# Block 0's score bursts on 32x64 array tiles: 16 full bursts in place of 18, with the output products half way between them

## The chip, the cores and the metric

The kernel runs on one core of a Trainium2 chip. The metric is device time in microseconds (us), taken by the median of several runs. The engines are PE (TensorE, matrix products), PEld (its weight loads, which overlap the products), DVE (VectorE), ACT (ScalarE), POOL (GpSimd) and SP (SyncE, which issues transfers).

## The reference

It is one transformer layer for 2048 tokens of width 1024, in bf16: a sliding-window causal attention with 32 heads of width 32 and window 256, then a feed-forward part.

```python
def _A_ref(x, wqkv, wo):                       # x is layernormed
    H = 32; Dh = D // H; W = 256
    q, k, v = ...                              # from x @ wqkv
    scores = jnp.einsum("bhqd,bhkd->bhqk", q, k) * (Dh ** -0.5)
    mask = (i - j >= 0) & (i - j < W)          # i query, j key
    p = _softmax(jnp.where(mask, scores, -1e9))
    o = jnp.einsum("bhqk,bhkd->bhqd", p, v)
    return o.reshape(B, S, D) @ wo
h  = x + _A_ref(_layernorm(x), wqkv, wo)
h2 = h + silu(_layernorm(h) @ w1) @ w2
```

## The kernel before

The 2048 tokens are four blocks of 512. TensorE works through the dense products of the next block (Q, K, V), 192 products of 512 columns for a block. Between them, in bursts, it computes the attention scores of the block before, and in pieces the attention outputs. A head group is four heads; their contractions are 32 long, so four row tiles of the array hold one head each. A burst fills two tiles in PSUM, the memory that TensorE writes: `sc[0]` and `sc[1]`, each with 512 columns for two heads (the text calls them the score banks). ScalarE takes the exponential into SBUF, GpSimd masks the triangles there, and TensorE later multiplies by V.

Block 0 has no keys before it, and had its own code: chunks of 128 keys by 128 queries, strung together over head groups, four to a burst.

```python
def first_stream(n_groups):
    bursts, where = [], {}
    for g in range(n_groups):
        for kt, q in ((0, 0), (0, 1), (0, 2), (1, 1), (1, 2), (1, 3), (2, 2), (2, 3), (3, 3)):
            if not bursts or len(bursts[-1]) == 4:
                bursts.append([])
            ...
def scores_first(n):
    ...                                       # nq: chunks in a row with the same keys
            for hh in range(4):
                r0 = hh * DH
                nc.tensor.matmul(
                    sc[hh // 2][:, hh % 2, ch * P:(ch + nq) * P],
                    lhsT=kT[0][r0:r0 + DH, g, kt * P:(kt + 1) * P],
                    rhs=qT[0][r0:r0 + DH, g, q0 * P:(q0 + nq) * P],
                    start=True, stop=True, tile_position=(r0, 0))
    for pair in range(2):
        e = ebuf[(2 * n + pair) % 12]          # a ring of six bursts
        nc.scalar.activation(out=e, in_=sc[pair], func=ACT.Exp, scale=scale)
        ...                                    # masks on GpSimd
```

An output piece (18 products of 33 columns: two heads, four query tiles) ran directly behind a burst:

```python
def between(kt):                               # called ahead of every dense product
    k, m = count
    if m * len(first_bursts) >= k * 192:
        run_late()
        scores_first(k)
        if pending:
            pending.pop(0)()
        ...
```

Blocks 1 to 3 already used 64-key halves on 32x64 tiles (`scores_xy`, with a burst of 128-key chunks, `scores_c`, for every second head group), a ring `xy_ring` of four bursts, a ring `c_ring` of three groups, and pieces half way between bursts.

The softmax here doesn't subtract the row's maximum and nothing guards it: scores larger than these inputs give would overflow.

## Time and profile before

| | before |
|---|---|
| time, median | 693.77 us (3 runs, 693.46 to 695.77); 693.63 us with three more |
| TensorE busy | 687.3 us, 99% of the span of 691.9 us |
| ScalarE, GpSimd busy | 240.8 us (35%), 161.8 us (23%) |
| stage of block 0 (first burst to first burst of the next stage) | 55.64 us |
| in it | 192 dense products, 18 bursts, 14 output pieces |

Read it so: with TensorE busy all the time, a stage is as long as the list of TensorE's instructions in it. The timeline gives each term by the difference of two starts. The lines are in the prediction below.

### The profile page before, as it was taken

To read this page: it belongs to the slowest core of one execution; us is meant where nothing else is said; L and a number is where in the kernel's file an instruction comes from. 1 tells how busy PE (TensorE), PEld (TensorE's weight loads), DVE (VectorE), ACT (ScalarE), POOL (GpSimd) and SP (SyncE) were. 2 spreads that over 40 slices of the span, in tenths; PEclk is the share of its full clock that TensorE was granted. 3 is DMA by queue.
4 is the path that set the end of the run, shared out by engine and by line. 5 is a ranking of instruction groups with operands and counts; after the bars stand their busy time and mean duration, and the time that the engine had idled before them with its cause. 6 is when DMAs were issued, how large, how long until landed. Compare 5 with 4: busy or idle time off the path is not lost.

```text
span 691.9 us, 13823 instructions
## 1 busy us (share of the span) xinstructions
PE 687.3 (99%) x5859; PEld 330.1 (48%) x5859; DVE 292.5 (42%) x616; ACT 240.8 (35%) x400; POOL 161.8 (23%) x295
## 2 busy tenths in 40 slices
PE   8999999999999999999999999999999999999998
PEld 3444445555555555544444444444444444444445
DVE  6267646744444449543315133343133251333111
ACT  4326656666766676521310033300133100233000
POOL 1007666656666665500000000000000000000000
PEclk9999999999999999999999999999999999999999
DMA  7732231236462999971023410023200023100110
GB/s 243 259 60 72 33 93 54 26 63 174 81 131 18 228 248 276 228 267 46 16 76 109 98 38 1 1 91 70 84 0 1 17 94 94 39 1 1 30 39 24
DMA packets 76462, 60.93 MB, mean 88 GB/s; under 512 B 50288, under 2 KB 60528, under 8 KB 76400
## 3 DMA queue, kind: packets, MB, share of 16 engines
q1 hardware_dynamic: 76256, 59.78, 33.1%
q8 instruction: 46, 0.75, 0.5%
q10 hardware_dynamic: 144, 0.26, 0.1%
q14 instruction: 16, 0.13, 0.1%
HBM read 39.85 MB, written 8.39 MB: 70 GB/s over the span
## 4 chain that ended last, share of the span: by engine, by line
PE 99%; DMA 0%; DVE 0%; issue 0%
PE hacc L615 19%; PE hacc L652 17%; PE acc L250 16%; PE acc L652 10%; PE acc L615 9%; PE acc L240 8%; PE acc L271 7%; PE o_ps L377 4%; PE sc L302 3%; PE hacc L271 1%; PE o_ps L392 1%; PE sc L348 1%; PE sc L328 1%; DMA r_o<-in_A_x_dram 0%; PE tp L218 0%; DVE ln_st L171 0%
## 5 line engine op out<-in xcount | busy, mean ns | idle before, releaser
L368 POOL TENSOR_SCALAR_AFFINE_SELECT r_e<-r_e 128x512 bf16<-128x512 bf16 (+1 forms) x288 | 158.8, 570 | 125.7 <-ACT r_e L357 64.7
L652 PEld LDWEIGHTS <-r_a 128*128 128x128 bf16 x952 | 90.9, 98 | 103.0
L615 PEld LDWEIGHTS <-r_w 128*128 128x128 bf16 x896 | 87.5, 98 | 105.0
L652 PE MATMUL hacc<-r_a 128*128 128x512 bf16 (+2 forms) x616 | 122.5, 360 | 0.0
L615 PE MATMUL hacc<-r_e,r_w 128*128 128x512 bf16 x456 | 100.9, 379 | 0.0
L314 ACT ACTIVATE r_e<-sc 128x768 bf16<-128x768 f32 x96 | 78.2, 814 | 48.3 <-PE sc L302 48.3
L624 ACT ACTIVATE r_n<-hacc 128x512 f32<-128x512 f32 x30 | 17.9, 597 | 178.9 <-PE hacc L615 178.9
L652 PE MATMUL acc<-r_a 128*128 128x512 bf16 x336 | 74.0, 379 | 0.0
L250 PEld LDWEIGHTS <-r_w 128*128 128x128 bf16 x512 | 45.0, 97 | 47.3 <-issue 0.2
L252 DVE CAST r_a<-acc 128x512 bf16<-128x512 f32 x56 | 38.6, 690 | 57.1 <-PE acc L250 56.9
L250 PE MATMUL acc<-r_t,r_w 128*128 128x512 bf16 x256 | 61.7, 379 | 0.0
L250 PE MATMUL acc<-r_w 128*128 128x512 bf16 x256 | 59.9, 379 | 0.0
L271 PE MATMUL acc<-r_o,r_a 128*128 128x512 bf16 x208 | 51.9, 379 | 0.0
L615 PE MATMUL acc<-r_e,r_w 128*128 128x512 bf16 x216 | 49.1, 379 | 0.0
L377 PEld LDWEIGHTS <-r_e 128*128 128x128 bf16 x1152 | 37.8, 96 | 14.2
L357 ACT ACTIVATE r_e<-sc 128x1024 bf16<-128x1024 f32 x36 | 34.9, 1021 | 21.2 <-PE sc L348 20.1
L377 PE MATMUL o_ps<-r_a,r_e 128*128 128x33 bf16 x1152 | 38.3, 178 | 0.0
L667 DVE SCALAR_TENSOR_TENSOR r_t<-hacc,r_t 128x512 bf16<-128x512 f32 (+2 forms) x22 | 14.0, 635 | 56.4 <-PE hacc L652 56.4
L315 ACT ACTIVATE r_e<-sc 128x256 bf16<-128x256 f32 x96 | 37.4, 390 | 0.0
L667 DVE SCALAR_TENSOR_TENSOR r_t<-acc,r_t 128x512 bf16<-128x512 f32 x12 | 8.3, 691 | 64.2 <-PE acc L652 64.2
L625 DVE SCALAR_TENSOR_TENSOR r_a<-r_n,hacc 128x512 bf16<-128x512 f32 x30 | 20.6, 688 | 33.0 <-ACT r_n L624 33.0
L615 PE MATMUL hacc<-r_a,r_w 128*128 128x512 bf16 x144 | 32.9, 379 | 0.0
(75 smaller groups left out, 529.0 us busy)
## 6 DMA issues: line engine op xcount, KB each, us to landing
r_w<-in_B_w_dram SPq DMA_DIRECT2D x8, 896.0 KB, 5.5
r_a<-in_B_w_dram SPq DMA_DIRECT2D x7, 1024.0 KB, 7.8
r_w<-in_A_wqkv_dram SPq DMA_DIRECT2D x6, 1024.0 KB, 8.6
h_dram<-r_t SPq DMA_DIRECT2D x16, 256.0 KB, 3.3
r_t<-h_dram SPq DMA_DIRECT2D x16, 256.0 KB, 2.9
out_dram<-r_t SPq DMA_DIRECT2D x31, 128.0 KB, 1.7
r_o<-in_A_x_dram SPq DMA_DIRECT2D x15, 256.0 KB, 3.6
r_e<-h_dram SPq DMA_DIRECT2D x3, 1024.0 KB, 5.7
```

Source lines behind the costliest of these rows:

```text
L240: nc.tensor.matmul(acc, lhsT=lnT_b[b % 2][:, kt, j * P:(j + 1) * P], rhs=wv[:, kt, c * 512:(c + 1) * 512], start=(kt == 0), stop=(kt == KT ...
L250: nc.tensor.matmul(acc, lhsT=wqk[:, kt, col0:col0 + P], rhs=lnT_b[b % 2][:, kt, :], start=(kt == 0), stop=(kt == KT - 1))
L252: copy(out=(qT, kT)[which][b][:, g, :], in_=acc)
L271: nc.tensor.matmul(acc, lhsT=qT[b][:, g, j * P:(j + 1) * P], rhs=wo[:, g, c * 512:(c + 1) * 512], start=(g == 0), stop=(g == G - 1))
L314: nc.scalar.activation(out=tri[:, :, :, 64:256], in_=both, func=ACT.Exp, scale=scale)
L315: nc.scalar.activation(out=e[:, 1024:1280].rearrange("p (h q) -> p h q", q=P), in_=bank[:, :, 192:320], func=ACT.Exp, scale=scale)
L357: nc.scalar.activation(out=e, in_=sc[pair], func=ACT.Exp, scale=scale)
L368: nc.gpsimd.affine_select(out=dst, in_=src, pattern=[[0, n] for n in dst.shape[1:-1]] + [[sgn, P]], compare_op=ALU.is_ge if upper else ALU ...
L377: nc.tensor.matmul(o_ps[pair][:, qt * 2 + hh, 0:VW], lhsT=chunk_of(i, bank, piece, pair, hh), rhs=v[:, b * 4 + kt, g * 4 + pair * 2 + hh, ...
L615: nc.tensor.matmul(acc, lhsT=w1[:, kt, ft * P:(ft + 1) * P], rhs=ln2T[b][:, kt, :], start=(kt == 0), stop=(kt == KT - 1))
L652: nc.tensor.matmul(acc[:, 0:c1 - c0], lhsT=gT[:, ft, j * P:(j + 1) * P], rhs=w2[ft // 4][:, ft % 4, c0:c1], start=(ft == 0), stop=(ft == F ...
L667: nc.vector.scalar_tensor_tensor(out=t_out[j % 2][:, c0:c1], in0=acc[:, 0:c1 - c0], scalar=0.5, in1=t_in[j % 2][:, c0:c1], op0=ALU.mult, o ...
```

## The change

Its intent is to give block 0 the scheme of the other blocks. With 64-key halves, columns that the mask removes need not be computed, and a head group fits into exactly two bursts of 512 columns, 16 in all. Pieces go half way between bursts. The deferred output transposes (`run_late`) also move: they are issued ahead of each eight dense products instead of ahead of each burst.

```diff
+CHUNKS_0 = [
+    [(0, "X", 0)],
+    [(0, "X", 1), (1, "Y", 0)],
+    [(0, "X", 2), (1, "Y", 1), (2, "X", 3)],
+    [(1, "Y", 2), (2, "C", 1), (3, "Y", 3)],
+]
-def first_stream(n_groups): ...
-    def scores_first(n): ...
+    def scores_0(g, odd):
+        q0 = odd * P
+        parts = [
+            (odd, 0, q0, q0 + 320, 0), (odd, 1, q0, q0 + 384, 0),
+            (odd + 2, 0, q0 + 256, 448, 320), (odd + 2, 1, q0 + 320, 448, 384),
+        ]
+        if odd:
+            parts = [(a, h, f, min(t, 512), c) for a, h, f, t, c in parts[:2]] + [
+                (3, 0, 384, 512, 320), (3, 1, 448, 512, 384), (2, 0, 448, 512, 448), (2, 1, 448, 512, 448)]
+        for step in range(0, len(parts), 2):
             for hh in range(4):
+                for t, half, qa, qb, col in parts[step:step + 2]:
+                    r0 = hh * DH
+                    k0 = t * P + half * 64
+                    nc.tensor.matmul(
+                        sc[hh // 2][half * 64:half * 64 + 64, hh % 2, col:col + qb - qa],
+                        ..., tile_position=(r0, half * 64),
+                    )
         for pair in range(2):
+            e = xy_ring[(g % 2 * 2 + odd) * 2 + pair][:, 0:1024].rearrange("p (h q) -> p h q", q=512)
+            nc.scalar.activation(out=e[:, :, 0:256], in_=sc[pair][:, :, 0:256], ...)
+            nc.scalar.activation(out=e[:, :, 320:512], in_=sc[pair][:, :, 256:448], ...)
+            nc.scalar.activation(out=c_ring[...], in_=sc[pair][:, :, 448:512], ...)
+            select(...)  # three masks of 256 columns
-    def attn_out_first(g, pair): ...
     class Stream:
         def __init__(self, b):
+            self.behind = 2 if b else 1
+            pending.extend(coming)
+            coming.clear()
         def between(self, kt):
-            if self.seen * 20 >= self.done * 192:
+            if self.seen * self.n >= self.done * 192:
                 self.bursts[self.done]()
                 self.done += 1
-            if self.seen * 40 >= (self.given * 2 + 1) * 192:
+            if self.seen * self.n * 2 >= (self.given * 2 + 1) * 192:
                 if pending:
                     pending.pop(0)()
-                coming.append(...)
-                if len(coming) > 2:
+                coming.append(self.pieces[self.given])
+                if len(coming) > self.behind:
                     pending.append(coming.pop(0))
...
-    def between(kt): ...
+    stream = Stream(0)
```

More of the change, by code (lines that the diff above doesn't have):

```diff
@@ L32 @@
 ]
-SPLIT = [(0, 8), (8, 16), (16, 21), (21, 27), (27, 32)]
-def first_stream(n_groups):
-    bursts, where = [], {}
-    for g in range(n_groups):
-        for kt, q in ((0, 0), (0, 1), (0, 2), (1, 1), (1, 2), (1, 3), (2, 2), (2, 3), (3, 3)):
-            if not bursts or len(bursts[-1]) == 4:
-                bursts.append([])
-            where[g, kt, q] = (len(bursts) - 1, len(bursts[-1]))
-            bursts[-1].append((g, kt, q))
-    return bursts, where
+CHUNKS_0 = [
[4 more added lines that the diff above has]
+]
+SPLIT = [(0, 8), (8, 16), (16, 21), (21, 27), (27, 32)]
 @with_exitstack
@@ L125 @@
     w2 = [view(r_a, w2_off + 4096 * s, 4, D) for s in W2_SLOT]
-    ebuf = [view(r_e, 1024 * i, 2, 512) for i in range(12)]
     c_ring = view(r_e, 0, 3, 4, 256)
@@ L160 @@
     make_identity(nc, ident[:])
-    warm = ebuf[0]
+    warm = view(r_e, 0, 2, 512)
     nc.vector.memset(warm, 0.0)
@@ L281, in chunk_of @@
             return c_ring[:, (i + 1) % 3, pair * 2 + hh, piece * P:(piece + 1) * P]
-        c0 = 1024 + hh * P if piece == 2 else hh * 512 + (piece - piece // 3) * P
+        if i < G:
+            c0 = hh * 512 + piece * P
+        else:
+            c0 = 1024 + hh * P if piece == 2 else hh * 512 + (piece - piece // 3) * P
         return xy_ring[(i % 2 * 2 + "XY".index(bank)) * 2 + pair][:, c0:c0 + P]
-    first_bursts, first_where = first_stream(G)
     def scores_xy(b, g, odd):
@@ L337, in scores_c @@
                                  in_=sc[pair].rearrange("p h (n q) -> p n h q", q=256), func=ACT.Exp, scale=scale)
-    def scores_first(n):
-        ch = 0
-        while ch < 4:
-            g, kt, q0 = first_bursts[n][ch]
-            nq = 1
-            while ch + nq < 4 and first_bursts[n][ch + nq] == (g, kt, q0 + nq):
-                nq += 1
-            for hh in range(4):
-                r0 = hh * DH
-                nc.tensor.matmul(
-                    sc[hh // 2][:, hh % 2, ch * P:(ch + nq) * P],
-                    lhsT=kT[0][r0:r0 + DH, g, kt * P:(kt + 1) * P],
-                    rhs=qT[0][r0:r0 + DH, g, q0 * P:(q0 + nq) * P],
-                    start=True, stop=True, tile_position=(r0, 0),
-                )
-            ch += nq
-        for pair in range(2):
-            e = ebuf[(2 * n + pair) % 12]
-            nc.scalar.activation(out=e, in_=sc[pair], func=ACT.Exp, scale=scale)
-            for ch, (g, kt, q) in enumerate(first_bursts[n]):
-                if kt != q - 1:
-                    mask(e, ch, 1, kt == q)
@@ L362, in mask @@
-    def mask(e, c0, n, upper):
-        for_each = e[:, :, c0 * P:(c0 + n) * P].rearrange("p h (c q) -> p h c q", q=P)
-        select(for_each, for_each, upper)
+    def scores_0(g, odd):
[8 more added lines that the diff above has]
+        for step in range(0, len(parts), 2):
+            for hh in range(4):
+                for t, half, qa, qb, col in parts[step:step + 2]:
[3 more added lines that the diff above has]
+                        sc[hh // 2][half * 64:half * 64 + 64, hh % 2, col:col + qb - qa],
+                        lhsT=kT[0][r0:r0 + DH, g, k0:k0 + 64],
+                        rhs=qT[0][r0:r0 + DH, g, qa:qb],
+                        start=True, stop=True, tile_position=(r0, half * 64),
+                    )
+        for pair in range(2):
+            e = xy_ring[(g % 2 * 2 + odd) * 2 + pair][:, 0:1024].rearrange("p (h q) -> p h q", q=512)
+            nc.scalar.activation(out=e[:, :, 0:256], in_=sc[pair][:, :, 0:256], func=ACT.Exp, scale=scale)
+            nc.scalar.activation(out=e[:, :, 320:512], in_=sc[pair][:, :, 256:448], func=ACT.Exp, scale=scale)
+            nc.scalar.activation(out=c_ring[:, (g + 1) % 3, pair * 2:pair * 2 + 2, 128 + 64 * odd:192 + 64 * odd],
+                                 in_=sc[pair][:, :, 448:512], func=ACT.Exp, scale=scale)
+            select(e[:, :, 0:P], e[:, :, 0:P], True)
+            select(e[:, :, 256:384], e[:, :, 320:448], False)
+            select(e[:, :, 384:512], e[:, :, 384:512], True)
@@ L375, in attn_out @@
             pair, qt, hh = n // 8, n // 2 % 4, n % 2
-            for m, (kt, bank, piece) in enumerate(CHUNKS[qt]):
+            chunks = (CHUNKS if b else CHUNKS_0)[qt]
+            for m, (kt, bank, piece) in enumerate(chunks):
                 nc.tensor.matmul(
@@ L380, in attn_out @@
                     rhs=v[:, b * 4 + kt, g * 4 + pair * 2 + hh, :],
-                    start=(m == 0), stop=(m == 2),
+                    start=(m == 0), stop=(m == len(chunks) - 1),
                 )
@@ L384, in attn_out @@
                 attn_norm(i, pair)
-    def attn_out_first(g, pair):
-        for qt in range(4):
-            for hh in range(2):
-                kts = range(max(0, qt - 2), qt + 1)
-                for kt in kts:
-                    n, ch = first_where[g, kt, qt]
-                    nc.tensor.matmul(
-                        o_ps[pair][:, qt * 2 + hh, 0:VW],
-                        lhsT=ebuf[(2 * n + pair) % 12][:, hh, ch * P:(ch + 1) * P],
-                        rhs=v[:, kt, g * 4 + pair * 2 + hh, :],
-                        start=(kt == kts[0]), stop=(kt == qt),
-                    )
-        attn_norm(g, pair)
-        if pair == 1:
-            late.append(lambda: attn_transpose(0, g))
     def attn_norm(i, pair):
@@ L428, in __init__ @@
         def __init__(self, b):
-            self.b, self.bursts, self.done, self.given, self.seen = b, [], 0, 0, 0
+            self.bursts, self.pieces, self.done, self.given, self.seen = [], [], 0, 0, 0
+            self.behind = 2 if b else 1
+            pending.extend(coming)
+            coming.clear()
             for g in range(0, G, 2):
-                self.bursts += [lambda g=g: scores_c(b, g)]
-                self.bursts += [lambda g=g, k=k, o=o: scores_xy(b, g + k, o) for k in range(2) for o in range(2)]
+                if b:
+                    self.bursts += [lambda g=g: scores_c(b, g)]
+                    self.bursts += [lambda g=g, k=k, o=o: scores_xy(b, g + k, o) for k in range(2) for o in range(2)]
+                    self.pieces += [lambda g=g, s=s: attn_piece(b, g, *s) for s in SPLIT]
+                else:
+                    self.bursts += [lambda g=g, k=k, o=o: scores_0(g + k, o) for k in range(2) for o in range(2)]
+                    self.pieces += [lambda g=g, k=k: attn_piece(b, g, k, k + 8) for k in range(0, 32, 8)]
+            self.n = len(self.bursts)
         def between(self, kt):
-            if self.seen * 20 >= self.done * 192:
+            if self.seen * self.n >= self.done * 192:
                 self.bursts[self.done]()
                 self.done += 1
-            if self.seen * 40 >= (self.given * 2 + 1) * 192:
+            if self.seen * self.n * 2 >= (self.given * 2 + 1) * 192:
                 if pending:
                     pending.pop(0)()
-                coming.append(lambda b=self.b, n=self.given: attn_piece(b, n // 5 * 2, *SPLIT[n % 5]))
-                if len(coming) > 2:
+                coming.append(self.pieces[self.given])
+                if len(coming) > self.behind:
                     pending.append(coming.pop(0))
@@ L523 @@
     pending, coming = [], []
-    count = [0, 0]
-    def between(kt):
-        k, m = count
-        if m * len(first_bursts) >= k * 192:
-            run_late()
-            scores_first(k)
-            if pending:
-                pending.pop(0)()
-            for g in range(G):
-                if first_where[g, 3, 3][0] == k:
-                    pending.extend([lambda g=g: attn_out_first(g, 0), lambda g=g: attn_out_first(g, 1)])
-            count[0] += 1
-        count[1] += 1
-    dense = [lambda j=j, c=c: v_group(1, j, c, dve, between) for j in range(4) for c in range(2)]
-    dense += [lambda w=w, g=g: qk_group(1, w, g, dve, between) for g in range(G) for w in range(2)]
+    stream = Stream(0)
+    dense = [lambda j=j, c=c: v_group(1, j, c, dve, stream.between) for j in range(4) for c in range(2)]
+    dense += [lambda w=w, g=g: qk_group(1, w, g, dve, stream.between) for g in range(G) for w in range(2)]
     for n in range(24):
+        run_late()
         dense[n]()
@@ L546 @@
             turns.pop(0)()
-    assert not steps and not turns and count[0] == len(first_bursts)
+    assert not steps and not turns
     for b in range(2, NB):
```

## The prediction

> **What bounds the kernel now.** I read the head of the page first, then its chain, then the timeline of TensorE in the stage that the change touches, then the same stage's waits, and last the stage of block 1, which already works the way that block 0 is to work.
>
> ```profile
> PE 687.3 (99%) x5859; PEld 330.1 (48%) x5859; DVE 292.5 (42%) x616; ACT 240.8 (35%) x400; POOL 161.8 (23%) x295
> ...
> PE 99%; DMA 0%; DVE 0%; issue 0%
> ```
>
> TensorE is busy 99% of the span, and the chain that ended last is TensorE for 99% too. So time goes down only where TensorE's own instruction stream gets shorter, and goes up where that stream gets longer or has to wait. ScalarE (35%) and GpSimd (23%) matter only if they make TensorE wait.
>
> The stage of block 0 begins with its first burst of scores and ends at the first burst of block 1's stage. The timeline of TensorE (start, length, line, output and inputs, count) shows its rhythm:
>
> ```profile
> 50.58 0.40 PE L348 MATMUL sc<-r_a 32*128 32x384 bf16 x8
> 50.91 2.55 PE L240 MATMUL acc<-r_w,r_t 128*128 128x512 bf16 x11
> 53.39 0.40 PE L348 MATMUL sc<-r_a 32*128 32x256 bf16 x8
> ...
> 58.79 0.40 PE L348 MATMUL sc<-r_a 32*128 32x384 bf16 x8
> 59.12 0.62 PE L392 MATMUL o_ps<-r_a,r_e 128*128 128x33 bf16 x18
> 59.59 2.53 PE L240 MATMUL acc<-r_w,r_t 128*128 128x512 bf16 x11
> 62.06 0.40 PE L348 MATMUL sc<-r_a 32*128 32x128 bf16 x12
> ...
> 106.22 0.40 PE L328 MATMUL sc<-r_a 32*128 32x128 bf16 x16
> ```
>
> L240 and L250 are the dense products of block 1, L348 a burst, L392 an output piece (18 products of 33 columns). Lengths overlap, so I use starts. The stage lasts 106.22 - 50.58 = 55.64 us. In an undisturbed stretch 50 dense products take 10.8 us, 0.216 us each, so the stage's 192 take 41.5 us. A burst takes 0.33 us from its start to the next instruction's (50.58 to 50.91); 11 dense products need 2.38 us, but from 50.91 to 53.39 are 2.48 us, so about 0.10 us goes by in front of each burst. A burst is 0.43 us. A piece takes 59.59 - 59.12 = 0.46 to 0.47 us; fourteen of the sixteen run in this stage, two after it. Sum: 41.5 + 18 x 0.43 + 14 x 0.46 = 41.5 + 7.7 + 6.4 = 55.6 us. That is the whole stage: it has no stall that a better order could win back.
>
> The waits of this stage name no wait of TensorE's products. What is there is the other engines waiting for TensorE, and a small wait of a weight load:
>
> ```profile
> ACT r_e L357 <- PE sc L348: 20.1, 17, 1.5
> ...
> PEld L392 <- POOL r_e L368: 0.4, 2, 0.2
> ```
>
> **What the Trainium skill says.** "TensorEngine Tiling (Array Packing)", section Tiling Modes, Key Properties, says that a change of tiling mode drains TensorE and that tiles work independently. The trace agrees with both: 0.10 us is lost in front of a burst, and a burst that streams four times 512 columns on four row tiles takes 0.33 us where one dense product of 512 takes 0.216. "TensorE: Matmul & The Clock Gate", section Back-to-back issue gap, gives N/2.4 + 2.5 ns, so 216 ns for 512 columns; the trace has 216. The same page, Part 3, section The mechanism, says that products start and end strictly in program order; nothing in the trace before tests this, since its 64-key bursts have halves of equal length in every step, and I use it only as a risk below.
>
> **The change part by part.**
>
> *Fewer bursts.* Before, a head group has 9 chunks of 128 keys by 128 queries, 1152 columns a head; 72 chunks fill 18 bursts of 512 columns. After, 64-key halves skip what the mask removes, and a group needs two bursts of 512 columns: 16 bursts. At 0.43 us this removes 2 x 0.43 = 0.86 us of TensorE. Most of it isn't streaming: 512 columns are 0.213 us, the rest is going into the small tiles and out.
>
> *Dearer bursts.* The 16 bursts run on 32x64 tiles and have 16 products (even) or 24 (odd), 320 in all where 168 were. Block 1's stage prices such a burst:
>
> ```profile
> 123.10 1.24 PE L240 MATMUL acc<-r_w 128*128 128x512 bf16 x5
> 124.27 0.43 PE L302 MATMUL sc<-r_a 32*64 32x320 bf16 x24
> 124.62 1.25 PE L240 MATMUL acc<-r_w 128*128 128x512 bf16 x5
> 125.71 0.61 PE L377 MATMUL o_ps<-r_a,r_e 128*128 128x33 bf16 x18
> 126.17 0.38 PE L240 MATMUL acc<-r_w 128*128 128x512 bf16 x1
> ```
>
> Five dense products end at 123.10 + 1.08 = 124.18, so 0.09 us in front, then 0.35 to 0.36 us: 0.45 us for 24 products and also 512 columns a half. That is 0.02 dearer than 0.43. The even burst has fewer products but unequal halves (320 and 384 columns, then 192 and 128). If products must start in order, a head's 192-column product can't start before its neighbour's second half does at column 384, and it ends at 576 instead of 512: 64 columns or 0.027 us more. So 0.45 to 0.47 us a burst, and 16 x 0.02 to 16 x 0.04 = 0.3 to 0.6 us back.
>
> *Outputs moved.* The pieces keep their size: per pair 2 x (1 + 2 + 3 + 3) = 18 products, 288 in all, and again 14 in the stage and two handed over. In front of them now stand dense products. The same lines show a piece of 18 there: 126.17 - 125.71 = 0.46 us, with the five dense before it at 1.09 instead of 1.08. So moving costs or wins under 0.01 us a piece; the burst's exit is paid towards a dense product instead.
>
> *ScalarE.* A burst had two exponentials of 1024 columns (1.94 us together, 51.01 to 52.95); now it has six, of 512, 384 and 128 columns twice. Block 1's four (768 and 256 twice) run from 118.87 to about 120.93, 2.06 us: 0.06 us for each further instruction. Six would take about 2.17 us (estimate). They start some 0.6 us after the burst's start (118.28 to 118.87), so the score banks are free 2.8 us after it. Bursts will stand 12 x 0.216 + 0.45 = 3.04 us apart without a piece and 3.5 us with one. TensorE doesn't wait.
>
> *GpSimd.* 96 masks of 256 columns before (6 of 9 chunks, 2 pairs, 8 groups), 96 after (3 x 2 x 16), at 0.42 us: 2.5 us a burst, inside 3.04 us. The mask results are wanted 1.5 burst intervals after their burst, over 4.5 us; pair 0's masks should be done after 0.6 + 1.1 + 1.3 = 3.0 us.
>
> *Sum.* 0.86 away, 0.3 to 0.6 back, at most 0.1 for the pieces: 0.2 to 0.5 us less, 0.4 taken. 693.77 - 0.4 = 693.4 us, 0.06% of the time.
>
> **Rivals.**
> 1. ScalarE becomes the stage's bound through its two score banks, which are not doubled. For it: block 1's stage shows such a stall. Where two bursts stood close, the second took 0.65 us instead of 0.36:
>
> ```profile
> 112.35 0.43 PE L302 MATMUL sc<-r_a 32*64 32x320 bf16 x24
> 112.71 2.12 PE L240 MATMUL acc<-r_w 128*128 128x512 bf16 x9
> 114.76 0.72 PE L302 MATMUL sc<-r_a 32*64 32x320 bf16 x24
> 115.41 1.25 PE L240 MATMUL acc<-r_w 128*128 128x512 bf16 x5
> ```
>
> Their starts lie 2.41 us apart, and 0.29 us of stall makes the shortest possible distance 2.70 us. Against it: with two more exponentials that becomes about 2.8 us, and the new bursts are never under 3.0 apart. If I am wrong by 0.3 us a burst, 16 bursts cost 5 us and the time is 698. That stall itself stays, as block 1's stage begins with the same two pieces and the same gap.
> 2. Ring or mask waits: the results now lie in a ring of four bursts, not six. Against it: the last piece that reads a slot runs half an interval (over 1.5 us) before the burst that refills it, and masks have over 1 us to spare. A few waits of 0.2 us make 694 to 695.
> 3. The move wins more, since the piece no longer directly follows a burst: 0.1 us won at each of 14 pieces would be 1.4 us more, so 692. Against it: a piece costs 0.46 us in both places.
>
> **Range and chances.** All terms are a few tenths of a microsecond; the three runs before span 693.46 to 695.77. From the sum, with run-to-run spread and a little for rival 2, I take 692.6 to 694.4. 2% is 13.9 us, a quarter of the whole stage: neither 18 bursts at 0.43 us nor rival 1 reaches it.
>
> **What would show it.** In the profile after: 16 bursts of 16 and 24 products, 3.04 us apart at first and 3.5 later; each 0.35 to 0.38 us from start to next start; pieces of 0.46 us; the stage 55.1 to 55.4 us long, against 55.64; summed busy time of ScalarE up, with waits for TensorE still in front of it; no wait of TensorE for ScalarE or GpSimd. I am wrong if a burst takes over 0.5 us, if a stall like the one at 114.76 shows in this stage, or if the stages of blocks 1 to 3 change length.

## The result, and the profile after

The changed kernel takes 693.19 us (median of 6 runs, 692.97 to 693.49), against 693.63 us of the kernel before (6 runs, 693.46 to 695.77). The ratio is 0.9989, with a 95% interval of 0.9976 to 1.0002. A ratio is the mean time of one kernel's runs over that of the other's of the same rounds, so it isn't quite the ratio of the medians. By the clock alone this is the same. The timeline is exact enough to say more.

The head of the page and of its chain, after:

```profile
PE 686.3 (99%) x6011; PEld 331.3 (48%) x6011; DVE 291.6 (42%) x616; ACT 240.9 (35%) x460; POOL 160.4 (23%) x295
...
PE 99%; DMA 1%; DVE 0%; issue 0%
```

TensorE has 152 products more and is busy 1.0 us less. Its timeline in the stage of block 0 (start, length, line, output and inputs, count), L350 being a burst and L378 a piece:

```profile
50.92 0.42 PE L350 MATMUL sc<-r_a 32*64 32x320 bf16 x16
51.27 2.76 PE L235 MATMUL acc<-r_w,r_t 128*128 128x512 bf16 x12
53.97 0.43 PE L350 MATMUL sc<-r_a 32*64 32x320 bf16 x24
...
58.69 0.61 PE L378 MATMUL o_ps<-r_a,r_e 128*128 128x33 bf16 x18
59.14 1.46 PE L235 MATMUL acc<-r_w,r_t 128*128 128x512 bf16 x6
60.53 0.43 PE L350 MATMUL sc<-r_a 32*64 32x320 bf16 x24
...
106.12 0.40 PE L324 MATMUL sc<-r_a 32*128 32x128 bf16 x16
```

The stage lasts 106.12 - 50.92 = 55.20 us, 0.44 less than before. A burst takes 0.35 to 0.36 us from its start to the next start, a piece 0.45 us. Bursts stand 3.05 us apart without a piece and 3.5 us with one. No product waits. What follows the stage is as long as before: 691.8 - 106.12 = 585.7 us, and 691.9 - 106.22 = 585.7 us, as far as the spans' one decimal tells.

One thing hides the gain in these two profiles: the stage starts 0.34 us later after (50.92 against 50.58). The first 128x128 transposes on TensorE show where this comes from, in the timeline of before and then of after:

```profile
6.70 1.05 PE L218 MATMUL tp<-ident,r_o 128*128 128x128 bf16 x8 [0.27 <-DVE r_o L199]
```

```profile
7.04 1.05 PE L213 MATMUL tp<-ident,r_o 128*128 128x128 bf16 x8 [1.09 <-DVE r_o L194]
```

They wait for the layernorm of the first rows and begin 0.34 us later. In the ten other profiles the stage starts anywhere from 50.34 to 50.85 us. So the profiles of these kernels differ by up to 0.58 us before any line that the change touches, and I compare lengths of stages from here on. Whether the slower runs without a profile (up to 695.77 us) also differ there isn't shown.

ScalarE's work on one burst after (the burst starts at 60.53):

```profile
61.06 0.60 ACT L358 ACTIVATE r_e<-sc 128x512 bf16<-128x512 f32 x1 [1.38 <-PE sc L350]
61.55 0.48 ACT L359 ACTIVATE r_e<-sc 128x384 bf16<-128x384 f32 x1
...
62.93 0.33 ACT L360 ACTIVATE r_e<-sc 128x128 bf16<-128x128 f32 x1
```

The six take 2.20 us, from 61.06 to 63.26, and leave the score banks free 2.73 us after the burst's start. In the view of waits ScalarE still waits for TensorE (three numbers: us in total, times, longest), not the other way round:

```profile
ACT r_e L358 <- PE sc L350: 20.4, 16, 1.5
```

The small wait of weight loads for GpSimd (0.4 us before) isn't in the list any more. The stall at the start of block 1's stage is still there, at 114.65 to 115.28 instead of 0.36 us:

```profile
112.25 0.43 PE L298 MATMUL sc<-r_a 32*64 32x320 bf16 x24
...
114.65 0.70 PE L298 MATMUL sc<-r_a 32*64 32x320 bf16 x24
115.28 1.25 PE L235 MATMUL acc<-r_w 128*128 128x512 bf16 x5
```

### The profile page after: what moved, and what is told of

It is laid out like the page before. It is cut to its first block, busy times and chain, and to the rows that moved or that the text cites. A ratio compares the mean times of both kernels' runs of the same rounds, so it can differ in the third digit from the quotient of the medians.

```text
span 691.8 us, 14227 instructions
## 1 busy us (share of the span) xinstructions
PE 686.3 (99%) x6011; PEld 331.3 (48%) x6011; DVE 291.6 (42%) x616; ACT 240.9 (35%) x460; POOL 160.4 (23%) x295
## 4 chain that ended last, share of the span: by engine, by line
PE 99%; DMA 1%; DVE 0%; issue 0%
PE hacc L597 19%; PE hacc L634 17%; PE acc L245 17%; PE acc L634 10%; PE acc L597 9%; PE acc L235 8%; PE acc L266 7%; PE o_ps L378 5%; PE sc L298 3%; PE hacc L266 1%; PE sc L350 1%; PE sc L324 1%; DMA r_o<-in_A_x_dram 1%; PE tp L213 0%; DVE ln_st L166 0%; DVE r_o L194 0%
## 5 line engine op out<-in xcount | busy, mean ns | idle before, releaser
L634 PEld LDWEIGHTS <-r_a 128*128 128x128 bf16 x952 | 90.9, 98 | 103.0
L245 PE MATMUL acc<-r_t,r_w 128*128 128x512 bf16 x256 | 63.4, 379 | 0.0
L378 PEld LDWEIGHTS <-r_e 128*128 128x128 bf16 x1440 | 47.4, 96 | 17.9
L378 PE MATMUL o_ps<-r_a,r_e 128*128 128x33 bf16 x1440 | 48.1, 178 | 0.0
L266 PEld LDWEIGHTS <-r_a 128*128 128x128 bf16 x256 | 21.8, 97 | 22.3
```

Source lines behind the costliest of these rows:

```text
L245: nc.tensor.matmul(acc, lhsT=wqk[:, kt, col0:col0 + P], rhs=lnT_b[b % 2][:, kt, :], start=(kt == 0), stop=(kt == KT - 1))
L266: nc.tensor.matmul(acc, lhsT=qT[b][:, g, j * P:(j + 1) * P], rhs=wo[:, g, c * 512:(c + 1) * 512], start=(g == 0), stop=(g == G - 1))
L378: nc.tensor.matmul(o_ps[pair][:, qt * 2 + hh, 0:VW], lhsT=chunk_of(i, bank, piece, pair, hh), rhs=v[:, b * 4 + kt, g * 4 + pair * 2 + hh, ...
L634: nc.tensor.matmul(acc[:, 0:c1 - c0], lhsT=gT[:, ft, j * P:(j + 1) * P], rhs=w2[ft // 4][:, ft % 4, c0:c1], start=(ft == 0), stop=(ft == F ...
```

## The experiments

My theory was that the stage is TensorE's list and nothing else: two bursts go (-0.86 us), the others become a little dearer, and moving the pieces costs nothing. The rivals were that the gain comes from the move, that the small tiles themselves are cheaper, and that ScalarE's bank turnaround or the ring bounds the stage. Ten kernels ran. "Stage" is block 0's, from the trace; "before" is the kernel before in the same rounds.

| run | median us | before | ratio | stage us |
|---|---|---|---|---|
| the change | 693.19 | 693.63 | 0.9989 | 55.20 |
| e1 pieces behind bursts | 693.29 | 693.59 | 0.9992 | 55.19 |
| e2 small tiles only | 694.24 | 693.59 | 1.001 | 56.10 |
| e3 bursts cut in two | 698.12 | 693.59 | 1.0064 | 59.42 |
| e4 loops swapped | 693.06 | 693.59 | 0.9992 | 55.20 |
| e5 one piece held back (wrong result) | 693.46 | 693.86 | 0.9995 | 54.75 |
| e6 one exponential twice | 693.76 | 693.86 | 0.9998 | 55.79 |
| e7 two exponentials twice | 702.08 | 693.86 | 1.012 | 63.67 |
| e8 e4 and e5 (wrong result) | 693.66 | 693.86 | 1.0 | 54.75 |
| e9 gap moved to the first interval | 693.21 | 693.99 | 0.9987 | 55.20 |
| e10 the change again | 693.52 | 693.99 | 0.9992 | 55.21 |

### e1: the move undone

```diff
-            if self.seen * self.n * 2 >= (self.given * 2 + 1) * 192:
+            if self.seen * self.n * 2 >= (self.given * 2 + (self.behind == 2)) * 192:
```

> The changed kernel with the pieces of output products put back directly behind their bursts (same pieces, same lag in pieces). My theory: where a piece stands costs TensorE nothing, 0.46 us in both places, so the stage of block 0 stays at 55.2 us within 0.1 and the time at 693.2 within 0.2. Rival: the gain of the change comes from the move; then the stage is 55.6 us or longer and the time is back at 693.6.

The first burst of the stage and of the next one, in the timeline of e1:

```profile
50.80 0.42 PE L350 MATMUL sc<-r_a 32*64 32x320 bf16 x16
...
105.99 0.40 PE L324 MATMUL sc<-r_a 32*128 32x128 bf16 x16
```

The stage is 55.19 us, 0.01 from the change. The move is worth nothing by itself, and the rival falls.

### e2: the small tiles alone

The kernel before, with its 18 bursts of the same chunks.

```diff
+                for k0 in (0, 64):
-                    sc[hh // 2][:, hh % 2, ch * P:(ch + nq) * P],
+                        sc[hh // 2][k0:k0 + 64, hh % 2, ch * P:(ch + nq) * P],
-                    lhsT=kT[0][r0:r0 + DH, g, kt * P:(kt + 1) * P],
+                        lhsT=kT[0][r0:r0 + DH, g, kt * P + k0:kt * P + k0 + 64],
-                    start=True, stop=True, tile_position=(r0, 0),
+                        start=True, stop=True, tile_position=(r0, k0),
```

> The kernel before with its same 18 bursts of 128x128 chunks, but every product cut into two 64-key halves on 32x64 tiles (336 products instead of 168). My theory: a burst becomes 0.02 us dearer (0.35 to 0.36 us from start to next start, instead of 0.33), so the stage grows from 55.64 to about 56.0 us and the time by 0.3 to 0.4 us. Rival: the small tiles are no dearer, or cheaper, by themselves; then the stage stays at 55.6 or falls.

The timeline of e2, a burst (L349) and the piece behind it:

```profile
62.29 0.43 PE L349 MATMUL sc<-r_a 32*64 32x128 bf16 x24
62.65 0.62 PE L393 MATMUL o_ps<-r_a,r_e 128*128 128x33 bf16 x18
```

The burst takes 0.36 us where the same chunks took 0.33. The stage is 56.10 us, so 18 bursts cost 0.46 us more, 0.026 each. The small tiles alone are a loss. They pay only because they let 16 bursts hold what took 18: e1 also has its pieces directly behind the bursts, and as a burst takes 0.36 us in both, 56.10 - 55.19 = 0.91 us is the price of two bursts at 0.455.

### e3: every burst cut in two

```diff
-        for step in range(0, len(parts), 2):
+        for step in (0,) if stage == 0 else range(2, len(parts), 2):
...
-        for pair in range(2):
+        for pair in range(2 if stage else 0):
...
         def between(self, kt):
+            while self.rest:                 # the second part, one dense product later
+                self.rest.pop()()
```

> The changed kernel with every burst cut in two: its first eight products, one dense product of block 1, then the rest and the exponentials. Columns streamed stay the same; 16 more entries into the small tiles and exits from them. My theory, that most of a burst's cost is going in and out: 0.10 us in front and about 0.14 us behind for each, 16 x 0.24 = 3.8 us more, stage 59 us, time 697. Rival: a burst costs what it streams (512 columns, 0.21 us); then the cut costs under 1 us.

The timeline of e3 in one even burst:

```profile
57.12 0.37 PE L350 MATMUL sc<-r_a 32*64 32x320 bf16 x8
57.42 0.39 PE L235 MATMUL acc<-r_w,r_t 128*128 128x512 bf16 x1
57.74 0.28 PE L350 MATMUL sc<-r_a 32*64 32x192 bf16 x8
57.95 1.25 PE L235 MATMUL acc<-r_w,r_t 128*128 128x512 bf16 x5
```

The stage grew by 4.22 us, 0.26 for each cut. The first part streams 384 columns, 0.16 us at the dense rate of 0.216 us for 512, and takes 0.30 us. The second streams 192, 0.08 us, and takes 0.21 to 0.22. An uncut burst streams 512, 0.216 us, and takes 0.355. Each time some 0.14 us lie on top, and 0.10 us in front (57.42 + 0.216 to 57.74). So going into the small tiles and out costs 0.24 us, whether the part streams 192, 384 or 512 columns. This is the price as a whole: e3 doesn't tell a drain of TensorE from weight loads that start late, or from issuing the small products one after another. The expected 0.24 didn't count that two halves of unequal length now both cost their longest, 384 + 192 = 576 columns: 0.027 us more, and 16 x 0.267 = 4.27 us. That last term is argued from the sum. The rival (a burst costs what it streams) falls.

### e4: the loops of a burst swapped

```diff
-            for hh in range(4):
-                for t, half, qa, qb, col in parts[step:step + 2]:
+            for t, half, qa, qb, col in parts[step:step + 2]:
+                for hh in range(4):
```

> The changed kernel with the two inner loops of a burst swapped: within a step all four heads of the lower half first, then all four heads of the upper half. If products start strictly in order, the unequal halves no longer hold each other up, and a burst gets up to 64 columns, 0.027 us, shorter: stage 55.2 to 54.8 us, time 0.4 us less. Rival: order within a burst doesn't matter, the stage stays at 55.2 us within 0.05.

The stage is 55.20 us, the same. The risk that I had put up for uneven halves, 0.027 us a burst, doesn't show: the 16-product burst takes 0.36 us in both orders. The trace of the change shows why. Here are the products at 64.18 to 64.222 us by shape, in the second part of the even burst that starts at 64.03:

```profile
L350 PE MATMUL sc<-r_a 32*64 32x384 bf16 x4 | 0.4, 345 | 0.0
L350 PE MATMUL sc<-r_a 32*64 32x320 bf16 x4 | 0.3, 318 | 0.0
L350 PE MATMUL sc<-r_a 32*64 32x192 bf16 x4 | 0.3, 241 | 0.0
```

The program alternates products of 192 and of 128 columns. All four of 192 have started by then and none of 128; the trace has those from 64.225 us on. So starts didn't keep program order between the halves, and no half held the other up. The median of 693.06 is no gain; this profile's stage started 0.58 us earlier than the change's.

### e5 and e8: one piece held back, a mistake of mine

```diff
-                if pending:
+                if pending and (self.behind == 2 or self.given < 15):
```

> The changed kernel with one output piece held back at the end of block 0's stage: 13 pieces run there and three are handed over, so that no interval at the start of block 1's stage is without a piece. My theory: the 0.28 us stall of the third 32x64 burst of block 1's stage comes from the score banks not being free, because the bursts stand only 2.4 us apart; with a piece between them they stand over 2.7 us apart and the stall is gone: time 0.25 to 0.3 us less than the changed kernel, 692.9. Rival: the stall comes from something else at that place (the ring's slots); then it stays, and the time with it.

> The changed kernel with both the swapped loops of a burst and the held-back piece. If both theories hold and the gains add: 0.4 + 0.28 = 0.7 us less than the changed kernel, 692.5 us, and better than both kernels. If neither does, 693.2.

Both gave a wrong result (relative error 0.067), which I hadn't intended. The held-back piece belongs to head group 6 and reads its `c_ring` slot, (6 + 1) % 3 = 1. The first burst of block 1's stage writes slots 0 and 1 in program order ahead of it. The trace of e5 shows the piece (L378) broken where it needs that slot:

```profile
106.75 0.48 PE L378 MATMUL o_ps<-r_a,r_e 128*128 128x33 bf16 x13
107.82 0.29 PE L378 MATMUL o_ps<-r_a,r_e 128*128 128x33 bf16 x5 [0.58 <-ACT r_e L332]
```

It waits 0.58 us for the exponentials that overwrite what it wants. Nothing was unordered, so nothing was a race; it read later data. What still can be read: the third 32x64 burst of that stage (start 115.07, next start 115.43) takes 0.36 us, without its stall. But the broken piece takes 1.21 us (106.75 to the next start at 107.96) instead of 0.45, so more than the 0.28 us won was lost. Block 0's stage is shorter in both runs only because it holds one piece fewer.

### e6 and e7: more exponentials, to find ScalarE's bound

```diff
+            for _ in range(1 + pair):          # e7: range(2)
                 nc.scalar.activation(out=e[:, :, 0:256], in_=sc[pair][:, :, 0:256], func=ACT.Exp, scale=scale)
```

> The changed kernel with one exponential of 512 columns done twice in each burst (pair 1 only): 0.48 us more of ScalarE a burst. My theory: the shortest distance of bursts goes from about 2.8 to about 3.27 us; the two intervals without a piece (3.05 us) get a stall of some 0.2 us each, the others (3.50 us) none: 0.4 us more, stage 55.6 us. Rival: ScalarE already bounds this stage, then each of 16 bursts gets 0.48 us: 7.7 us more.

> The same exponential done twice for both pairs: 0.96 us more of ScalarE a burst. My theory: the shortest distance becomes about 3.75 us, over all intervals: 2 x 0.7 + 14 x 0.25 = 4.9 us more, stage 60 us, each burst waiting for ScalarE. If ScalarE never bounded (another buffer hid it), the stage stays at 55.2 us.

e6 adds 0.59 us, where I had expected 0.4: the second and third burst, which have no piece in front, take 0.63 and 0.68 us, and the next four take 0.36 to 0.37, as without the addition. e7 adds 8.47 us, where I had expected 4.9. One burst of e7, from its timeline:

```profile
69.74 0.35 PE L350 MATMUL sc<-r_a 32*64 32x320 bf16 x4
...
70.25 0.42 PE L350 MATMUL sc<-r_a 32*64 32x320 bf16 x20 [0.15 <-ACT r_e L361]
...
70.81 1.23 ACT L359 ACTIVATE r_e<-sc 128x512 bf16<-128x512 f32 x2 [0.61 <-PE sc L350]
```

Four products go into the first pair's banks, then TensorE waits for the second pair's. The mechanism is as expected, and my size for the repeated exponential was off: two into the same place take 1.23 us, so the second adds 0.63 us. In the trace it waits for the semaphore that the first one raises, which a different exponential doesn't. I had taken 0.48, near what an exponential adds when a different one follows it (0.49 us, 61.06 to 61.55 above). The shortest distance is then 2.73 + 2 x 0.63 = 4.0 us, and the bursts at 69.74, 73.75 and 77.79 stand 4.01 and 4.04 apart. For e6 it is about 3.4, between 3.05 and 3.5, which is why only the intervals without a piece paid. So, by the 2.73 us, the changed kernel keeps an estimated 0.3 us of slack in its shortest interval and 0.8 us in the others.

### e9 and e10: the stall of block 1's stage removed

```diff
-            self.behind = 2 if b else 1
+            self.behind, self.skip = 2 if b else 1, b == 1
...
-                if pending:
+                if pending and not (self.skip and self.given == 0):
```

> The changed kernel with the gap without a piece moved: at the start of block 1's stage the first interval gets none (after the 128-key burst, whose exponentials end 2.4 us after its start), the second and third get the two pieces left over from block 0. No ring slot is read later than its refill this time, so the result must be right. My theory: no two bursts stand closer than their exponentials need, the 0.28 us stall of the third 32x64 burst goes and none comes: from the first burst of block 1's stage to the fourth 32x64 burst 11.75 us instead of 12.03, time 0.28 us less than the changed kernel of the same rounds. Rival: a stall comes at the second burst instead, then nothing is won.

> The changed kernel unaltered, to have it in the same rounds as the run above: stage of block 0 at 55.20 us, time 0.4 us under the kernel before, stall of 0.28 us in block 1's stage present. If the stage lengths of TensorE are what differs, and the rest of the spread is in the start of the program, the start of the stage will again differ by tenths of a microsecond from run to run while the stage's length does not.

e9 is correct. Its timeline at the start of block 1's stage:

```profile
106.05 0.40 PE L324 MATMUL sc<-r_a 32*128 32x128 bf16 x16
106.38 2.33 PE L235 MATMUL acc<-r_w 128*128 128x512 bf16 x9
...
114.58 0.43 PE L298 MATMUL sc<-r_a 32*64 32x320 bf16 x24
114.94 1.25 PE L235 MATMUL acc<-r_w 128*128 128x512 bf16 x5
...
117.81 0.43 PE L298 MATMUL sc<-r_a 32*64 32x320 bf16 x24
```

From the first burst of the stage to the fourth 32x64 burst are 11.76 us, against 12.03 in the change and in e10. The burst at 114.58 takes 0.36 us, and no burst took over the stall. The median is 693.21 us, 0.31 below e10 in the same rounds. So e9 is the quickest of the kernels by its trace, 0.27 us under the change and about 0.7 under the kernel before. By the clock its ratio is 0.9987 (interval 0.9974 to 1.0001).

e10 repeats the change: stage 55.21 us, median 0.47 under the kernel before.

## Why the prediction was right

The time was 693.19 us against 693.4 predicted, in the range of 692.6 to 694.4. Against the forecast of 0.4 us less, the medians differ by 0.44 and the stage by 0.44. The range says little, as the time before lies in it too, and so does the agreement of the medians, as the interval of the ratio includes 1. The test of the argument is the stage: forecast at 55.1 to 55.4 us, measured at 55.20. Step by step:

- **The bound.** The stage is TensorE's list: shown by the lengths adding up before and after (41.5 + 16 x 0.455 + 14 x 0.45 = 55.1 us after), and by e3, where cuts in that list come out in the time (+4.22 us in the stage). The formula that the prediction quotes for a dense product is, on its page, the one for an isolated product. For a sustained stream the same section gives about 131 ns; the stream here has 216.
- **Fewer bursts.** I took 2 x 0.43 = 0.86 us. Dividing what dense products and pieces leave over gives (55.64 - 41.5 - 6.4) / 18 = 0.43 us before. At the small tiles' price, e2 against e1 has 0.455 us for each of the two. That most of it is entry and exit was a step of the argument; e3 shows a little over half, 0.24 us of about 0.45.
- **Dearer bursts.** I took 0.02 to 0.04 us each. e2 has 0.026. 16 x 0.026 = 0.42 us back, and 0.86 - 0.42 = 0.44 is the result.
- **Uneven halves.** The upper end of that term rested on a start in program order. e4 shows no such cost; the even burst takes 0.36 us like the odd one, and its products don't start in program order. The risk didn't come true; it had only widened the range.
- **The move.** Under 0.01 us a piece; e1 gives 0.01 us for all.
- **ScalarE.** Six exponentials were estimated at 2.17 us and took 2.20; banks free at 2.8, measured 2.73. That no burst waits for them held, and e6 and e7 show how far off the bound is. One line was wrong: I wrote that the summed busy time of ScalarE would go up. By my own figures it should not have, as 16 x 2.17 = 34.7 and 18 x 1.94 = 34.9 us; it went from 240.8 to 240.9 us in the whole span. The time doesn't depend on it.
- **Ring and masks.** No wait for them appeared. The prediction's reading passed over one wait of ScalarE for GpSimd before (1.1 us); it isn't there after, and TensorE waited for neither. Pair 0's masks were to be done 3.0 us after the burst; GpSimd's six run from 61.73 to 64.18, so the first three end about 2.5 us after it.
- **The stall at block 1's start** stayed, as said, and e9 shows that the distance of the bursts was its cause.

What stays open: why the first layernorm of the program ends up to 0.58 us earlier or later. No run varied it.

## What to carry to other kernels

When one engine is busy all the time, price a change as a list: instructions gone and come, each by the difference of two starts in a stage that already works in the new way. Going into small array tiles and out has a price for itself (0.24 us here, more than the 0.216 us that the burst streams), so pack small products into as few and as full bursts as the score banks allow, and don't expect the smaller tile to win by itself. A rhythm of bursts has a shortest period, set by how soon the consumer frees the banks; look for the one interval that is shorter, as its stall can be moved away for nothing.

## What the Trainium skill lacked or had wrong

- "TensorEngine Tiling (Array Packing)", section Tiling Modes, says that a change of mode drains TensorE but has no price. Here it was 0.10 us in front of a burst and 0.14 us on top of what it streams, together 0.24 us (e3). What share of it is the drain isn't shown.
- "TensorE: Matmul & The Clock Gate", section LDWEIGHTS, makes a weight load proportional to its columns, so 64 columns should take half of 128. Here loads of 64 columns on 32x64 tiles have a median of 104 ns, and loads of 128 columns on 32x128 tiles 93 ns. These are the lengths that the profile records; why they differ so isn't shown.
- The same page, Part 3, section The mechanism, has products start and end strictly in program order. Here starts didn't keep program order across tiles: four 192-column products started by 64.22 us and the 128-column ones between them in the program from 64.225 us on. A cost for uneven halves (0.027 us a burst) didn't appear either: swapping the loops left the stage at 55.20 us (e4).
- "ScalarE: Activation LUTs", section What ACT_TABLE_LOAD costs, says that back-to-back activations overlap by about 93 ns. In the burst at 60.53 different ones overlapped by 0.10 to 0.16 us (the first is 0.60 us long, and the next starts 0.49 us after it). The two of e7 (1.23 us, no overlap) are no measure of it, as there the second waits for the first's semaphore.
